# Weighted experts in 64x64 tiles: seven block products for both matrix products

## The chip, the cores and the metric

The kernel runs on one core of one Trainium2 chip. TensorE (PE) multiplies matrices into PSUM, VectorE (DVE) and ScalarE (ACT) work on PSUM and SBUF, GpSimd (POOL) on SBUF alone, and SyncE (SP) issues nearly all transfers (DMA). The metric is the time of one execution on the device in microseconds (us), the median of the runs.

## The reference

A linear attention feeds a mixture of eight experts whose weights come out of Sinkhorn iterations. N = 4352 tokens, D = 128, E = 8, F = 1024, all in float32.

```python
# attention: (4, 4, 1088, 32) inputs, features phi(x) = outer(S1 x, S2 x), 64 of them
num = q_p @ (k_p^T v);  den = q_p @ sum(k_p) + 1e-6
x = (num / den), heads side by side             # (4352, 128)
# experts
P = np.exp(x @ w_gate - max)
for _ in range(8):
    P /= P.sum(1, keepdims=True) + 1e-09
    P /= P.sum(0, keepdims=True) + 1e-09
    P *= N / E
for e in range(E):
    h = np.maximum(x @ w1[e], 0.0)              # (4352, 1024)
    out += P[:, e:e + 1] * (h @ w2[e])          # (4352, 128)
```

The weights P are positive, so `P * relu(x w1)` is the same as `relu((P x) w1)`.

## The kernel before

`xT` holds the attention's result with the 128 channels on the partitions and the tokens along the free dimension. The work of the experts is a list of `groups` (a stretch of tokens and a list of experts), and an item is one expert in one group. While the attention and the Sinkhorn iterations run on VectorE, TensorE is filled with plain items: experts 0 and 1 on tokens that need no weight yet; their sums are kept in `kept` and weighted later. The generator `steps()` yields after every step of expert work, and `fill(n)` runs some steps between two pieces of the other work.

The other items are weighted: `prepare_x` loads a row of P, broadcast to 128 partitions, and GpSimd multiplies the tokens by it (L682) ahead of the first product. Weighted groups of 768 tokens are three tiles of 256. `four` computes the first product directly (L918, ReLU on ScalarE, L922): four blocks of 128 hidden units by three tiles, each as two 128x64 matmuls on the two column halves of the array. `twenty` gives the second product (L1103) as 20 block products in place of 24, with sums of hidden blocks on VectorE (L982, L1002) and sums of weight blocks (`sums_of_four`, L246) that GpSimd computes once and SP stores and loads again (L234). The last group has two tiles of 256 and a scheme with seven products in place of eight (`two`, `seven`). The second products of a block are issued eight steps after its first products (`LAG`), between first products of later blocks, so that TensorE need not wait for ReLU and sums.

PSUM has eight banks: four rotate for first products (`aps`), four hold the sums of the second products (`mps`, tags s0 to s3). `load_w` brings an expert's w1 (L194) and w2 (L195, 512 KB each) through SP; the pool `wpool` has two buffers of each, so a load waits until the use before last of its buffer is over.

TensorE, VectorE and ScalarE run in the order in which the source issues (`manual_schedule(engines=...)`); SP and GpSimd are ordered by the scheduler, except where `keep_in_program_order` pins an instruction. Every engine carries out its instructions in its order; an instruction that waits holds up those behind it, and on SP these are transfers.

Of the kernel before, what the change touches and what calls it, by code (L numbers as in the profile page):

```python
# [50 lines left out]
def kernel(  # L51
# [33 lines left out]
    aps = ctx.enter_context(tc.tile_pool(name="aps", bufs=4, space=PSUM))  # L85
    mps = ctx.enter_context(tc.tile_pool(name="mps", bufs=1, space=PSUM))
    dram = ctx.enter_context(tc.tile_pool(name="dram", bufs=1, space=bass.MemoryType.DRAM))
# [103 lines left out]
    def load_w(e, sums=True, again=False):  # L191
        w1 = wpool.tile([P, F], F32, tag="w1", name="w1")
        w2 = wpool.tile([P, FO, DM], F32, tag="w2", name="w2")
        nc.sync.dma_start(out=w1, in_=moe_w1[e])  # L194
        nc.sync.dma_start(out=w2, in_=moe_w2[e].rearrange("(fo fi) d -> fi fo d", fi=P))  # L195
        return w1, w2, sums_of_two(e, w2, again) if sums else None

    def sums_of_two(e, w2, again=False):

        ws = wpool.tile([P, 4, FO // 2, H2], F32, tag="ws", name="ws")  # L200
        if e in stored:
            nc.sync.dma_start(out=ws, in_=stored[e])
            return ws
        a11, a21 = w2[:, 0::2, 0:H2], w2[:, 0::2, H2:DM]
        a12, a22 = w2[:, 1::2, 0:H2], w2[:, 1::2, H2:DM]
        keep_ = tc.keep_in_program_order if e < 2 else lambda x: x
        keep_(nc.gpsimd.tensor_tensor(ws[:, 0], a21, a22, op=Alu.add))
        keep_(nc.gpsimd.tensor_tensor(ws[:, 1], ws[:, 0], a11, op=Alu.subtract))
        keep_(nc.gpsimd.tensor_tensor(ws[:, 2], a11, a21, op=Alu.subtract))
        keep_(nc.gpsimd.tensor_tensor(ws[:, 3], a12, ws[:, 1], op=Alu.subtract))  # L210
        if again:
            stored[e] = dram.tile([P, 4, FO // 2, H2], F32, name=f"ws{e}")
            nc.sync.dma_start(out=stored[e], in_=ws)
        return ws

    stored, stored_four = {}, {}

    FOURS = (((5, 6), ((0, 0), (0, 2)), ((1, 0), (1, 2)), True),  # L220
# [7 lines left out]
    FORMS = [n for ns, *_ in FOURS for n in ns]  # L228

    def sums_of_four(e, w2):  # L230

        ws = pools[0].tile([P, len(FORMS), FO // 4, H2], F32, tag="ws4", name="ws4")
        if e in stored_four:
            nc.sync.dma_start(out=ws, in_=stored_four[e])  # L234
            return ws

        def blocks(bs):
            b = w2[:, bs[0][1]::4, H2 * bs[0][0]:H2 * (bs[0][0] + 1)].unsqueeze(1)
            if len(bs) == 1:
                return b  # L240
            step = (bs[1][1] - bs[0][1]) * DM + (bs[1][0] - bs[0][0]) * H2
            return AP(tensor=b.tensor, offset=b.offset, ap=[b.ap[0], [step, 2], *b.ap[2:]])

        c = 0
        for ns, x, y, off in FOURS:
            tc.keep_in_program_order(nc.gpsimd.tensor_tensor(ws[:, c:c + len(ns)], blocks(x), blocks(y),  # L246
                                                             op=Alu.subtract if off else Alu.add))
            c += len(ns)
        stored_four[e] = dram.tile([P, len(FORMS), FO // 4, H2], F32, name=f"ws4{e}")
        nc.sync.dma_start(out=stored_four[e], in_=ws)  # L250
        return ws


# [38 lines left out]
    first_w = load_w(0, False)  # L292
# [282 lines left out]
    def routing():  # L575
# [45 lines left out]
        for b in (1, 0, 2, 3):  # L621
# [10 lines left out]
    NT3 = 256  # L632

    groups = [(0, 256, 2, [0], False), (512, 288, 2, [0], False), (0, 256, 2, [1], False),
              *((1088 + 832 * i, 416, 2, [0], False) for i in range(3)), (3584, 384, 2, [0], False),
              (512, 384, 2, [1], False)]
    PLAIN = len(groups)


    DIRECT = (0,)
    for lo in (1280, 512, 2048, 2816, 3584):
        groups.append((lo, NT3, 3, list(range(2 if lo == 512 else 1, E)), True))
    groups.append((0, 256, 2, list(range(2, E)), True))
    assert sorted((lo, e) for lo, n, t, es, _ in groups for lo in range(lo, lo + n * t, 32) for e in es) == [
        (lo, e) for lo in range(0, N, 32) for e in range(E)]
    kept = [keep.tile([P, N], F32, name="kept0"), keep.tile([P, 1280], F32, name="kept1")]
    items = [(g, e) for g, group in enumerate(groups) for e in group[3]]
    loaded_w, sources, sums, parts, done = {}, {}, {}, {}, {}  # L650
# [5 lines left out]
    def tiles_of(j):  # L656
        return groups[items[j][0]][2]

    def prepare_w(j):
        g, e = items[j]  # L660
        three = groups[g][2] == 3
        if j == 0:
            loaded_w[j] = first_w
        elif items[j - 1][1] == e or not groups[g][4]:
            before = [i for i in range(j) if items[i][1] == e and i in loaded_w]
            loaded_w[j] = loaded_w[before[-1]] if before else load_w(e, False)
            if three and tiles_of(j - 1) == 2:
                loaded_w[j] = *loaded_w[j][0:2], sums_of_four(e, loaded_w[j][1])
        else:
            loaded_w[j] = load_w(e, not three, again=groups[g][4])  # L670
            if three:
                if g == len(groups) - 2 and e in groups[-1][3]:
                    sums_of_two(e, loaded_w[j][1], True)
                loaded_w[j] = *loaded_w[j][0:2], sums_of_four(e, loaded_w[j][1])

    def weights_of(e, lo, n, tag):
        pb = pools[0].tile([P, 3 * NT3], F32, tag=tag, name=tag)[:, 0:n]
        tc.keep_in_program_order(nc.sync.dma_start(out=pb, in_=pT[e:e + 1, lo:lo + n].to_broadcast([P, n])))
        return pb

    def weigh(out, x, pb):
        tc.keep_in_program_order(nc.gpsimd.tensor_tensor(out, x, pb, op=Alu.mult))  # L682

    def prepare_x(j):
        g, e = items[j]
        lo, n, t, es, weighted = groups[g]
        x = xT[:, lo:lo + t * n]
        if not weighted:
            sources[j] = x
            return  # L690
        xe = weights_of(e, lo, t * n, "xe")
        for sl in (slice(0, 512), slice(512, 768)) if j == first_weighted else (slice(0, t * n),):
            weigh(xe[:, sl], x[:, sl], xe[:, sl])
        sources[j] = xe

    first_weighted = next(j for j, (g, e) in enumerate(items) if g == PLAIN)

    def weigh_kept(g, i):

# [185 lines left out]
    LAG = 8  # L885
# [389 lines left out]
```

## Time and profile before

| | |
|---|---|
| runs | 920.46, 920.62 and 922.18 us; median 920.62 us |
| profiled execution | span 919.9 us, 19030 instructions |
| TensorE busy | 913.1 us, 99% |
| VectorE, ScalarE, GpSimd busy | 685.0 us (74%), 421.2 us (46%), 211.0 us (23%) |
| moved by DMA | 128.17 MB, 139 GB/s in the mean |

The profile is of one execution. Busy time is the time in which at least one instruction of an engine runs; the chain that ended last follows the end of the program back through what each instruction waited for. "PE" rows are matmuls, "PEld" rows weight loads. Line numbers are those of the kernel printed above.

### The profile page before, as it was taken

What the parts mean: (1) busy time and instruction counts of PE and PEld (TensorE: products, weight loads), DVE (VectorE), ACT (ScalarE), POOL (GpSimd) and SP (SyncE); (2) the same over time, 40 slices, a digit from 0 to 9 for tenths busy, and PEclk for the clock granted to TensorE, in tenths of its full rate; (3) what the DMA queues carried; (4) which work ended last, traced back from release to release, by engine and by line L of the source; (5) the groups of instructions that cost most, each with busy time, mean ns of one, the idle gap of its engine ahead of it and who ended that gap; (6) DMA issues with size and microseconds to landing.
All of it is one profiled execution on the core that took longest, in us unless ns stands there. A gap on an engine that the chain in (4) does not pass through costs nothing.

```text
span 919.9 us, 19030 instructions
## 1 busy us (share of the span) xinstructions
PE 913.1 (99%) x7510; PEld 596.8 (65%) x7510; DVE 685.0 (74%) x1173; ACT 421.2 (46%) x915; POOL 211.0 (23%) x212
## 2 busy tenths in 40 slices
PE   9999999999999999999999999999999999999997
PEld 5777544466666666666666666666666666668665
DVE  7678699888776798756985666967667986668665
ACT  2455465554444454444544444544445444446443
POOL 3121100076545412200210011110100352221220
PEclk9999999999999999999999999999999999999999
DMA  8995100213554535534364343464435556453650
GB/s 233 309 276 178 53 1 1 70 64 116 157 142 147 169 136 152 187 109 139 121 173 148 110 149 110 125 196 120 139 114 169 155 149 195 157 170 92 176 152 13
DMA packets 91306, 128.17 MB, mean 139 GB/s; under 512 B 25392, under 2 KB 69504, under 8 KB 86480
## 3 DMA queue, kind: packets, MB, share of 16 engines
q1 hardware_dynamic: 88384, 121.42, 42.7%
q0 software_dynamic: 1600, 5.36, 1.9%
q8 instruction: 59, 0.97, 0.4%
q10 hardware_dynamic: 1232, 0.16, 0.1%
q14 instruction: 31, 0.25, 0.1%
HBM read 107.88 MB, written 19.05 MB: 138 GB/s over the span
## 4 chain that ended last, share of the span: by engine, by line
PE 98%; DVE 1%; issue 0%; ACT 0%; POOL 0%; DVEq 0%; POOLq 0%
PE a L918 56%; PE s L1103 37%; PE a L351 1%; PE a L117 1%; PE a L466 1%; PE a L318 0%; PE s L380 0%; DVE hb L935 0%; PE a L430 0%; PE s L396 0%; PE a L500 0%; PE a L396 0%; DVE cs L606 0%; DVE rs L600 0%; DVE y L794 0%
## 5 line engine op out<-in xcount | busy, mean ns | idle before, releaser
L918 PE MATMUL a<-xe,w 128*64 128x256 f32 (+1 forms) x2560 | 692.1, 470 | 0.0
L918 PEld LDWEIGHTS a<-xe,w 128*64 128x64 f32 x2560 | 320.4, 137 | 112.8 <-issue 1.6
L1103 PE MATMUL s<-hb,ws 128*64 128x256 f32 (+3 forms) x1312 | 331.6, 395 | 0.2 <-DVE hb L935 0.2
L1103 PE MATMUL s<-hx,ws 128*64 128x256 f32 x1280 | 306.3, 379 | 0.0
L922 ACT ACTIVATE hb<-a 128x256 f32<-128x256 f32 (+4 forms) x408 | 195.0, 480 | 241.9 <-PE a L918 208.9
L922 ACT ACTIVATE hx<-a 128x256 f32<-128x256 f32 (+1 forms) x360 | 167.0, 464 | 213.6 <-PE a L918 191.3
L982 DVE TENSOR_TENSOR hb<-hb 128x512 f32<-128x512 f32 (+1 forms) x204 | 134.9, 671 | 100.9 <-ACT hb L922 97.0
L1103 PEld LDWEIGHTS s<-hb,ws 128*64 128x64 f32 x1312 | 158.4, 137 | 70.2 <-issue 14.2
L982 DVE TENSOR_TENSOR hx<-hx 128x512 f32<-128x512 f32 (+1 forms) x204 | 152.7, 759 | 59.8 <-ACT hx L922 54.7
L682 POOL TENSOR_TENSOR xe<-xT,xe 128x768 f32<-128x768 f32 (+2 forms) x41 | 85.0, 2074 | 481.6 <-DMA xe<-pT 371.3
L1103 PEld LDWEIGHTS s<-hx,ws 128*64 128x64 f32 x1280 | 154.5, 137 | 57.3
L1103 PE MATMUL s<-hb,w 128*64 128x256 f32 (+3 forms) x536 | 134.4, 408 | 0.0
L918 PE MATMUL a<-xT,w 128*64 128x416 f32 (+3 forms) x512 | 119.9, 463 | 0.0
L1103 PE MATMUL s<-hx,w 128*64 128x256 f32 x384 | 95.7, 380 | 0.0
L1103 PEld LDWEIGHTS s<-hb,w 128*64 128x64 f32 x536 | 60.5, 137 | 23.4 <-issue 6.5
L935 DVE TENSOR_TENSOR hb<-hb 128x416 f32<-128x416 f32 (+7 forms) x84 | 60.7, 723 | 18.7 <-ACT hb L922 14.8
L918 PEld LDWEIGHTS a<-xT,w 128*64 128x64 f32 x512 | 49.5, 137 | 25.1 <-issue 15.5
L246 POOL TENSOR_TENSOR ws<-w 128x256 f32<-128x256 f32 (+1 forms) x70 | 62.1, 920 | 5.4 <-DMA w<-in_moe_w_dram 4.0
L935 DVE TENSOR_TENSOR hx<-hx 128x256 f32<-128x256 f32 (+1 forms) x65 | 38.6, 598 | 24.7 <-ACT hx L922 23.6
L1103 PEld LDWEIGHTS s<-hx,w 128*64 128x64 f32 x384 | 46.1, 137 | 11.8 <-DVE hx L935 0.7
L982 DVE TENSOR_TENSOR pqg<-hb 128x512 f32<-128x512 f32 x68 | 46.5, 723 | 0.0
L982 DVE TENSOR_TENSOR pqg<-hx 128x512 f32<-128x512 f32 x68 | 36.4, 574 | 0.0
(181 smaller groups left out, 483.0 us busy)
## 6 DMA issues: line engine op xcount, KB each, us to landing
w<-in_moe_w_dram SPq DMA_DIRECT2D x82, 512.0 KB, 5.6
ws<-ws SPq DMA_DIRECT2D x34, 1024.0 KB, 5.0
xe<-pT SPq DMA_DIRECT2D x34, 384.0 KB, 4.0
ws<-ws SPq DMA_DIRECT2D x12, 512.0 KB, 4.3
ph<-qa SPq DMA_DIRECT2D x12, 288.0 KB, 5.0
rb<-qb SPq DMA_DIRECT2D x3, 1152.0 KB, 7.8
pb<-pT SPq DMA_DIRECT2D x6, 384.0 KB, 7.2
kx<-in_k_dram SPq DMA_DIRECT2D x4, 544.0 KB, 5.2
```

The costliest lines, as they stand in the source:

```text
L117: nc.tensor.matmul(warm[r][cols, 0:256], ones[rows, cols], ones[rows, 0:1].to_broadcast([64, 256]), start=True, stop=True, tile_position=( ...
L246: tc.keep_in_program_order(nc.gpsimd.tensor_tensor(ws[:, c:c + len(ns)], blocks(x), blocks(y), op=Alu.subtract if off else Alu.add))
L351: nc.tensor.matmul(pv[64 * s:64 * (s + 1), i], kp[0:n, H * t + h].rearrange("p i j -> p (i j)"), vx[0:n, slots[h], t, :], start=(t == 0 an ...
L466: nc.tensor.matmul(pn[64 * s:64 * (s + 1), t, 2 * i:2 * i + 2].rearrange("p h d -> p (h d)"), ph[:, i, s, 64 * t:64 * (t + 1)], kvs[b % 2] ...
L682: tc.keep_in_program_order(nc.gpsimd.tensor_tensor(out, x, pb, op=Alu.mult))
L918: nc.tensor.matmul(ph[sl], loaded_w[j][0][:, P * f + H2 * s:P * f + H2 * (s + 1)], sources[j][:, lo:hi], start=True, stop=True, tile_posit ...
L922: nc.scalar.activation(out=out, in_=ph, func=Act.Relu)
L935: nc.vector.tensor_tensor(out, a, b, op=Alu.subtract)
L982: nc.vector.tensor_tensor(out if not isinstance(out, tuple) else places(*out), places(*a), places(*b) if isinstance(b, tuple) else b, op=A ...
L1103: nc.tensor.matmul(sums[g][i][H2 * s:H2 * (s + 1), n * place:n * (place + 1)], w, x, start=c == 1, stop=c == per, tile_position=(0, H2 * s))
```

## The change

The plain items stay. `twenty`, `four` and the last group's scheme go, and after the plain items a new phase runs, `weighted()`, with all engines in the order of the source. Its items are nine groups `wgroups`, each of two tiles of n tokens (six of n = 256, two of 224, one of 192) with six or seven experts; every second group takes its experts in reverse order, so that the expert at a border stays. All matmuls are 64x64 with four positions in the array. An item is done in two halves s.

- First product: channels, hidden units and tokens are each cut in two, and seven products of blocks replace eight. `w1x` holds 4 raw blocks of w1 and 4 sums (`sum_forms`, GpSimd, at an expert's first use; then `store_forms` stores them, and `stored_forms` loads 1 MB of them and 512 KB of `ws`). `xf` holds the weighted tokens (`weigh`, GpSimd), a copy with the partition halves exchanged (two DMAs from SBUF to SBUF), and four sums (`sum_x`, VectorE). The products accumulate in two pairs of PSUM banks; the state in between is copied out or added (`firsts`).
- Second product: seven products again, with sums `ts` of hidden blocks (`seconds`), summed over an item's rounds and a group's experts in the four banks of `mps`. In the first weighted group the second product is plain, eight products.
- One round of `firsts` of half t and one of `seconds` of half t - 1 alternate on TensorE.
- A group's end: copies out of PSUM, a sum, an exchange of partition halves by DMA, nine small adds, the kept sums, transposes, stores; the VectorE part runs in pairs at `spare()`.

```diff
+    wgroups = [*((1280 + 512 * i, 256, list(range(1, E))) for i in range(6)),
+               (0, 224, list(range(2, E))), (448, 224, list(range(2, E))), (896, 192, list(range(2, E)))]
...
+    def stored_forms(e):
+        w1 = late[0].tile([P, 8, FORM], F32, tag="w1x", name="w1x")
+        w2 = wpool.tile([P, FO, DM], F32, tag="w2", name="w2")
+        ws = wpool.tile([P, 4, FO // 2, H2], F32, tag="ws", name="ws")
+        nc.sync.dma_start(out=w1, in_=form_stores[e][0])
+        nc.sync.dma_start(out=w2, in_=moe_w2[e].rearrange("(fo fi) d -> fi fo d", fi=P))
+        nc.sync.dma_start(out=ws, in_=form_stores[e][1])
+        return w1, w2, ws
...
+    def load_weights(i):
+        g, e = witems[i]
+        lo, n, _ = wgroups[g]
+        weights[i] = late[0].tile([P, 2 * NW], F32, tag="pb", name="pb")[:, 0:2 * n]
+        nc.sync.dma_start(out=weights[i], in_=pT[e:e + 1, lo:lo + 2 * n].to_broadcast([P, 2 * n]))
+
+    def weigh(i):
+
+        lo, n, _ = wgroups[witems[i][0]]
+        xf = sources[i] = late[0].tile([P, 8 * NW], F32, tag="xf", name="xf")[:, 0:8 * n].rearrange(
+            "p (b n) -> p b n", b=8)
+        nc.gpsimd.tensor_tensor(xf[:, 0:2].rearrange("p b n -> p (b n)"), xT[:, lo:lo + 2 * n], weights.pop(i),
+                                op=Alu.mult)
+        for s in range(2):
+            nc.sync.dma_start(out=xf[H2 * (1 - s):H2 * (2 - s), 2:4], in_=xf[H2 * s:H2 * (s + 1), 0:2])
+
+    def sum_x(i, part_):
+        xf = sources[i]
+        if part_ == 0:
+            nc.vector.tensor_tensor(xf[:, 4:6], xf[:, 1:4:2], xf[:, 0:2], op=Alu.subtract)
+        else:
+            nc.vector.tensor_tensor(xf[:, 6], xf[:, 3], xf[:, 4], op=Alu.subtract)
+            nc.vector.tensor_tensor(xf[:, 7], xf[:, 2], xf[:, 6], op=Alu.subtract)
+
+    def prepare(i):
+
+        if i < len(witems):
+            e = witems[i][1]
+            if i and witems[i - 1][1] == e:
+                forms[i] = forms[i - 1]
+            else:
+                forms[i] = stored_forms(e) if e in form_stores else raw_forms(e)
+
+    def begin(i):
+        if i >= 0:
+            store_forms(i)
+        else:
+            load_weights(0)
+        prepare(i + 1)
+        if i + 2 < len(witems):
+            load_weights(i + 2)
+        if i + 1 < len(witems):
+            weigh(i + 1)
+            if witems[i + 1][1] not in form_stores:
+                sum_forms(forms[i + 1])
+        if i >= 0:
+            weigh_kept(i)
...
+        def firsts(t):
...
+            def product(out, form, x, start, stop):
+                for r in range(2):
+                    rows = slice(H2 * r, H2 * (r + 1))
+                    for col in range(2):
+                        o = P * s + H2 * col
+                        nc.tensor.matmul(out[H2 * col:H2 * (col + 1), r], w1[rows, form, o:o + H2], xf[rows, x],
+                                         start=start, stop=stop, tile_position=(H2 * r, H2 * col), skip_group_check=True)
...
+            product(pa, 0, 0, True, True)
+            nc.scalar.copy(flat(p1, n), pa)
+            yield
+            product(pc, 4, 4, True, True)
+            nc.scalar.copy(flat(p5, n), pc)
+            yield
+            product(pa, 5, 6, False, True)
+            nc.scalar.copy(flat(u2, n), pa)
+            yield
+            product(pc, 7, 3, False, True)
+            add(h[:, 0], pc, u2)
+            relu(h[:, 0], h[:, 0])
+            yield
+            product(pa, 6, 5, False, True)
+            add(h[:, 2], pa, p5)
+            relu(h[:, 2], h[:, 2])
+            yield
+            product(pc, 2, 2, True, True)
+            add(h[:, 3], pc, p1)
+            if i + 1 < len(witems):
+                sum_x(i + 1, s)
+            spare()
+            if g == 0:
+                relu(h[:, 3], h[:, 3])
+            yield
+            product(pa, 3, 7, False, True)
+            relu(flat(h[:, 1], n), pa)
+            if g:
+                nc.vector.scalar_tensor_tensor(ts[:, 0:2], h[:, 3:4].to_broadcast([P, 2, 2 * n]), 0.0, h[:, 0:2],
+                                               op0=Alu.max, op1=Alu.subtract)
+                nc.vector.tensor_tensor(ts[:, 2], h[:, 1], ts[:, 0], op=Alu.subtract)
+                nc.vector.tensor_tensor(ts[:, 3], h[:, 2], ts[:, 2], op=Alu.subtract)
+            yield
...
+            for m, (x, y) in enumerate((((raw, (0, 0), h[:, 0], 0, 0), (raw, (0, 1), h[:, 2], 0, 0)),
+                                        ((form, (3,), h[:, 1], 0, 1), (form, (0,), ts[:, 0], 0, 1)),
+                                        ((form, (2,), ts[:, 1], 1, 0), (form, (1,), ts[:, 2], 1, 0)))):
+                for r in range(2):
+                    both(into(0, x[0](*x[1], r), x[2], r, *x[3:]), into(1, y[0](*y[1], r), y[2], r, *y[3:]))
+                    if last and m == 1 and r == 1:
+                        ended(g, 0)
+                    yield
+            both(into(0, raw(1, 1, 0), ts[:, 3], 0, 1, 1), into(1, raw(1, 1, 1), ts[:, 3], 1, 1, 1))
...
+        for t in range(len(todo) + 1):
+            if t < len(todo) and todo[t][1] == 0:
+                begin(todo[t][0])
+            f = firsts(t) if t < len(todo) else iter(())
+            s = seconds(t - 1) if t else iter(())
+            nothing_, open_ = object(), 2
+            while open_:
+                open_ = sum(next(x, nothing_) is not nothing_ for x in (f, s))
+        while leisure:
+            leisure.pop(0)()
...
-        pools.append(ctx.enter_context(tc.tile_pool(name="late", bufs=2)))
-        prepare_x(PLAIN)
-        fill(8)
-    for _ in work:
-        pass
+        late.append(ctx.enter_context(tc.tile_pool(name="late", bufs=2)))
+        begin(-1)
+        fill(7.5)
+        for _ in work:
+            pass
+        sum_x(0, 0)
+        sum_x(0, 1)
+    turning.close()
+    fps = ctx.enter_context(tc.tile_pool(name="fps", bufs=1, space=PSUM))
+    with tc.manual_schedule():
+        weighted()
```

More of the change, by code (lines that the diff above doesn't have):

```diff
@@ L676, in weights_of @@
[L676 to L694, printed above, removed]
@@ L1105, in into @@
+        nc.tensor.matmul(sums[g][i][H2 * s:H2 * (s + 1)], w, x, start=c == 1, stop=c == per,
+                         tile_position=(0, H2 * s))
         if c == per:
@@ L1108, in into @@
                 part(g, i)
-    def second(k, p):
-        into(items[blocks[k][0]][0], *p)
     def steps():
@@ L1137, in steps @@
                     loaded_w.update({i: w for i in loaded_w if items[i][1] == items[j + 1][1]})
[L1138 to L1145 removed]
+                step, sums_ = two(k)
+                products = eight if g in DIRECT else seven
+            for c in range(4):
                 if k < len(blocks):
@@ L1152, in steps @@
                 for b, p in todo.pop(t, ()):
-                    second(b, p)
+                    into(items[blocks[b][0]][0], *p)
                 if k < len(blocks) and c == 0:
@@ L1163, in steps @@
                         later.pop(0)()
-                elif later and (tiles == 3 or c % 2 or share > 0.9):
+                elif later and (c % 2 or share > 0.9):
                     later.pop(0)()
```

549 lines of the change are left out of this document (222 added, 327 removed), and 7 rows, old and new, of the table FOURS.

## The prediction, made before the changed kernel ran

> **What bounds the kernel now.** I read the page first: the busy times, then the chain that ended last, then the costliest groups.
>
> ```profile
> PE 913.1 (99%) x7510; PEld 596.8 (65%) x7510; DVE 685.0 (74%) x1173; ACT 421.2 (46%) x915; POOL 211.0 (23%) x212
> ...
> PE 98%; DVE 1%; issue 0%; ACT 0%; POOL 0%; DVEq 0%; POOLq 0%
> ...
> L918 PE MATMUL a<-xe,w 128*64 128x256 f32 (+1 forms) x2560 | 692.1, 470 | 0.0
> ```
>
> TensorE is busy for 913.1 us, the chain runs through it for 98%, and its main group never waited. So two things move the end: TensorE work taken away, and any wait put in front of TensorE. The mean of 470 ns is no price, since matmuls overlap; the price is the distance between starts, in TensorE's timeline near the end:
>
> ```profile
> 908.96 1.03 PE L1103 MATMUL s<-hx,ws 128*64 128x256 f32 x8
> 909.82 1.03 PE L1103 MATMUL s<-hb,w 128*64 128x256 f32 x8
> 910.68 0.38 PE L1103 MATMUL s<-hx,ws 128*64 128x256 f32 x1
> ```
>
> Eight instructions take 0.86 us. One matmul of the source is two instructions (the x2560 are 1280 calls), and two column halves run side by side, so a pair of 128x64 matmuls over 256 columns costs 0.43 us. I call that a round.
>
> **TensorE's work.** The weighted phase before has 34 items of 768 tokens, each of two blocks with 12 rounds of first and 10 of second products; 6 items of 512 tokens, four blocks of 4 + 3.5 rounds; and 2.5 rounds more that go into the last sums: 1496 + 180 + 2.5 = 1678.5 rounds, 721.8 us.
>
> Afterwards a round is four 64x64 matmuls. That four run at once only the warm-up shows, in the timeline of the start:
>
> ```profile
> 1.00 8.17 PE L117 MATMUL a<-ones 64*64 64x256 f32 x96 [1.00 <-POOL own L120]
> ...
> 5.75 0.25 PEld L117 LDWEIGHTS a<-ones 64*64 64x64 f32 x4 [0.18 <-issue]
> ...
> 6.17 0.25 PEld L117 LDWEIGHTS a<-ones 64*64 64x64 f32 x4 [0.18 <-issue]
> ...
> 6.60 2.11 PEld L117 LDWEIGHTS a<-ones 64*64 64x64 f32 x40 [0.18 <-issue]
> ```
>
> From 6.60 on, 40 loads take 2.11 us, 0.42 us for the eight instructions of four matmuls. I keep 0.43. A half item costs 7 rounds of first and 7 of second products (8 in the first group, whose second products are plain): 14 x 15 + 35 x 28 = 1190 rounds of 256 columns, 336 of 224 and 168 of 192, worth 1610 rounds, 692.3 us. TensorE's work falls by **29.5 us**, if nothing new waits.
>
> **The wait that the change adds.** Take item i with its halves A and B. At the start of A, `begin(i)` puts on SP's queue, in this order (the new region keeps every engine in the order written, SP and POOL too): w1's forms for item i+1, w2, the sums `ws`, the weights `pb` of item i+2, and only then the two transfers that swap the halves of `xf` for item i+1. w2 has two buffers. The one that item i+1 gets was item i-1's, and the second products of i-1's last half run between the first products of this very half A, down to A's last round. SP does wait for such releases; its own waits:
>
> ```profile
> SPq L234 <- PE s L1103: 153.4, 23, 7.7
> ...
> SPq L195 <- PE s L1103: 49.8, 30, 7.3
> ```
>
> L195 loads w2; it was held 30 times until second products let a buffer go. So SP will stand at w2 until the end of A (call it moment 0), and behind it stand `ws`, `pb` and the swaps. VectorE's program, which is in order, has `sum_x(i+1, 0)` after A's sixth round of first products, and that reads the swapped half. So VectorE stands from before moment 0 until the swap lands, and behind it stand the four sums `ts` of half A. TensorE does five rounds of half B (2.15 us) and then, in its third round of second products, needs the first of these sums.
>
> When does the swap land? SP's spacing and a burst with a like number of bytes are in SP's timeline, the windows beside it and the DMA issues:
>
> ```profile
> 490.09 0.32 SPq L678 DMA_DIRECT2D xe<-pT  x1
> 490.46 0.42 SPq L194 DMA_DIRECT2D w<-in_moe_w_dram  x1
> 498.67 0.32 SPq L234 DMA_DIRECT2D ws<-ws  x1
> 499.96 0.38 SPq L195 DMA_DIRECT2D w<-in_moe_w_dram  x1
> ```
> ```profile
> 499.50:500.00 0.50, 0.50 (x6) 0.29 (x4) 0.50 (x2) 0.38 (x1) 0.00 (x0) 1.00 0.55 66
> ...
> 505.00:505.50 0.50, 0.50 (x6) 0.35 (x4) 0.18 (x1) 0.00 (x0) 0.00 (x0) 1.00 0.11 33
> 505.50:506.00 0.50, 0.50 (x6) 0.28 (x4) 0.00 (x0) 0.39 (x1) 0.00 (x0) 1.00 0.00 0
> ```
> ```profile
> w<-in_moe_w_dram SPq DMA_DIRECT2D x82, 512.0 KB, 5.6
> ws<-ws SPq DMA_DIRECT2D x34, 1024.0 KB, 5.0
> ```
>
> The last columns of a window are the granted clock, the DMA share and GB/s. 1024 KB of sums and 512 KB of w2 kept the DMA engines busy until about 505.4, 6.7 us after the first issue. Afterwards the burst is w2 512, `ws` 512, `pb` 256 and the swaps 256 KB, the same total, with the swaps at its end. With 0.1 us for SP to wake, the landing is at 6.8 us. Bounds come from the tile `xd`, the transfer out of SBUF that this trace has, below with the rows of the engines' steps:
>
> ```profile
> DMA to landing us min/median/max: 2.4/3.3/7.9
> ```
> ```profile
> L982 DVE TENSOR_TENSOR hx<-hx 128x512 f32<-128x512 f32 x136 | 98.6, 725 | 47.4 <-ACT hx L922 44.2
> L335 DVE TENSOR_TENSOR kp<-ab 128x1024 f32<-128x1024 f32 x8 | 9.6, 1216 | 2.0 <-ACT ab L321 2.0
> L935 DVE TENSOR_TENSOR hx<-hx 128x256 f32<-128x256 f32 x42 | 20.9, 500 | 1.8 <-ACT hx L922 0.7
> ```
> ```profile
> L922 ACT ACTIVATE hx<-a 128x512 f32<-128x512 f32 x136 | 81.2, 597 | 103.4 <-PE a L918 85.4 <-DVE hb L982 13.7 <-DVE hx L982 3.3
> ```
> ```profile
> L682 POOL TENSOR_TENSOR xe<-xT,xe 128x512 f32<-128x512 f32 x7 | 10.2, 1451 | 124.9 <-PE s L1103 79.8 <-DMA xe<-pT 30.9 <-PE a L918 14.2
> ```
>
> Early end: the fifth issue, 0.1 + 4 x 0.37 = 1.6 us, and 2.4 us, so 4.0; late end: 7.9. I take 6.8, the precedent of the same size. Then VectorE does `sum_x` (512 wide, 0.73 us) and the first pair of `ts` (1024 wide, 1.22 us); with 0.2 us of handing over TensorE goes on at 8.95. It stopped at 2.15, so **6.8 us of idle TensorE in one item**; 4.0 by the early end, 7.9 by the late one.
>
> How many items? Of 59 preparations, 7 keep the expert across a border of groups, the 7 after them find the buffer free earlier, and so does the first. That leaves 44: 5 in the first group, 26 in the next five, 13 in the last three, where smaller tiles give about 6.6. In the first group no `ws` is loaded and no `ts` exists: the late step is the add of half B's first sum, needed after ten rounds (4.3 us) and ready at about 6.7; 3 us with the stores of the new forms in the same queue. Together 26 x 6.8 + 13 x 6.6 + 5 x 3 = **278 us**. Between `sum_x` and `ts` stand also up to two adds of a finished group, 0.4 to 0.5 us each, in about three stalled items after each of six borders: 18 x 0.85 = **15 us**.
>
> The rest hides: POOL's product ahead of the swap (1.45 us) is done while SP stands, and after the stop 23 rounds lie before the next moment 0, in which VectorE catches up. With that cover gone POOL's product would add its 1.45 us per item.
>
> **The clock.** An idle TensorE is clocked down, as the windows at the end show:
>
> ```profile
> 914.00:915.00 1.00, 0.93 (x9) 0.35 (x5) 0.93 (x4) 0.00 (x0) 0.00 (x0) 1.00 0.00 0
> 917.00:918.00 1.00, 0.00 (x0) 0.00 (x0) 0.00 (x0) 0.00 (x0) 0.00 (x0) 0.98 0.90 130
> 918.00:919.00 1.00, 0.00 (x0) 0.00 (x0) 0.00 (x0) 0.00 (x0) 0.00 (x0) 0.50 0.32 45
> ```
>
> The last matmul ends at 914.9 and the clock is halved at 918.0, 3 us later. The start shows the way back: groups of four came every 0.42 us (5.75, 6.17), and every 0.21 us only from 6.60 on, 5.6 us after the first matmul. A stop of 6.8 us is therefore followed by some 5.6 us at half speed, which loses 2.8 us: 39 x 2.8 = **109 us** (none for the first group's 3 us). Bounds: 0, if the clock should hold, and 39 x 3.4 if the way back took as long as the stop.
> The Trainium skill (TensorE: Matmul & The Clock Gate, Part 1) says that a free-running window of about 3.4 us decides: halved after one idle window, restored after one busy one. By that rule the slow stretch is 3.4 to 6.8 us, 5.1 in the mean, and the term 39 x 2.55 = 99 us in place of 109; this trace's 3 and 5.6 us agree with it.
>
> **The edges.** The phases no longer overlap. VectorE must do the last plain adds (about four) and `sum_x` before the second round, some 4.6 us for TensorE; the first half has no second products between its rounds and the last no first ones: 2.6 us. At the end, this is what now lies behind the last matmul:
>
> ```profile
> 913.69 1.24 PE L1103 MATMUL s<-hb,w 128*64 128x256 f32 x9
> ...
> 915.92 0.45 DVE L718 STREAM_TRANSPOSE yt<-y 128x256 f32<-128x256 f32 x1
> ```
>
> Before: 5.0 us from 914.93 to the span's end, 3.6 of them the stores. Afterwards: copies 1.0, a sum 0.5, a swap 3, nine adds 3.5, two adds and two transposes 1.4, stores 3.6: 13, so 8 us more. Edges: **15 us**.
>
> **The sum**, on the profiled execution of 919.9 us: 919.9 - 29.5 + 278 + 15 + 109 + 15 = 1307.4; the median of the runs is 0.7 us above that span, so **1308 us**.
>
> **Rivals.**
> - The swap is not late: were the slot of w2 free, or the swap issued ahead of it, so that it lands by moment 0, nothing stops. For it: POOL is 77% idle and SP's work per item is short. Against it: the 30 waits of L195. VectorE would then have 3 x 0.73 + 0.73 + 1.22 + 2 x 0.73 = 5.6 us in a half of 6.02, so TensorE stays the bound: 919.9 - 29.5 + 15 + 0.7 = 906 us, faster. It decides if the sums are ready at 2.15, that is, if the swap lands by 0.1 us after moment 0. Chance 0.05.
> - The stop is there, but the clock holds: 1199 us. For it: only one drop and one rise are in the trace, and 3 us is half the stop. Chance 0.15.
> - The swap doesn't queue behind the burst and lands at 4.0: a stop of 4.0 us, 39 x 2.8 = 109 us less, and a clock that drops in some stops only: 1090 to 1199, say 1150. For it: sixteen DMA engines take several transfers at once. Against: a total of 1.5 MB shares them. Chance 0.13.
> - Four tiles with four different inputs don't run at once (the warm-up streams a single repeated column): rounds of 0.86 us, 692 us more work and, as the sums are then needed at 4.3 us, stops of 4.7 us: about 1900 us. Chance 0.03.
>
> **How the numbers follow.** The forecast has 0.62 and spans 1210 to 1380: the late end gives 39 x 1.1 = 43 us more, slower VectorE steps some 20. The remaining 0.02 is for what I don't see. The range 1110 to 1380 holds the forecast, the held clock and most of the third rival. A measurement of this kernel can tell about 0.2% from no change. Faster by more: the first rival, 0.05. Within: 0.01. Slower: 0.94.
>
> **What would show it.** In the changed profile: SP's waits should list w2 behind TensorE's second products some 40 times at about 6 us; VectorE's longest waits should be for the DMA into `xf`, 44 times; TensorE's busy share should fall to about 60 to 70%, with stops once in every item of 20 to 22 us, at the third round of second products; granted clocks of 0.7 to 0.9 in the slices; rounds of 0.43 us between stops. Wrong would be: no such waits on `xf` (then 906), full clock in every slice (1199), rounds well over 0.43 at full clock.

## The result and the profile after

The changed kernel takes **1445.04 us** (median of 4 runs, 1438.3 to 1450.18); the kernel before took 920.58 us. The ratio is 1.568, 95% interval 1.564 to 1.573. The forecast was 1308 us: the direction was right, but the time lies 137 us above the forecast and 65 us above the top of the range.

The page of the changed kernel, where before TensorE stood at 99% and the chain ran through it for 98%:

```profile
span 1436.4 us, 35651 instructions
...
PE 1025.1 (71%) x15436; PEld 751.4 (52%) x15436; DVE 845.5 (59%) x1264; ACT 536.5 (37%) x993; POOL 163.6 (11%) x197
...
PEclk9999998998878897888889887978787879789777
...
PE 49%; DVE 21%; DMA 18%; SPq 6%; issue 4%; ACT 2%; POOL 0%; DVEq 0%; ACTq 0%; POOLq 0%
```

No engine is busy throughout, the clock dips in nearly every slice of the second phase, and VectorE and a transfer have joined the chain. The waits name them (engine and line, what was waited for; us in total, times, longest), first the engines, then SP:

```profile
DVE xf L905 <- DMA xf<-xf: 384.3, 44, 10.3
PE s L1051 <- DVE hb L1023: 361.6, 69, 10.7
```
```profile
SPq L855 <- PE s L1051: 125.8, 22, 7.7
SPq L855 <- PE pair L981: 111.5, 24, 7.1
```

L905 is `sum_x(i+1, 0)`: it waited for the swap 44 times, the number that the prediction counted. L855 loads w2: SP was held there 46 times. One item in the timeline (start, duration; in brackets the idle time before and what ended it):

```profile
704.45 0.40 SPq L855 DMA_DIRECT2D w<-in_moe_w_dram  x1
...
706.05 1.25 SPq L900 DMA_DIRECT2D xf<-xf  x2
...
706.28 0.59 PE L1051 MATMUL s<-hb,ws 64*64 64x256 f32 x2
713.38 0.69 DVE L905 TENSOR_TENSOR xf<-xf 128x512 f32<-128x512 f32 x1 [9.53 <-DMA xf<-xf]
...
714.35 1.18 DVE L1023 SCALAR_TENSOR_TENSOR hb<-hb 128x1024 f32<-128x1024 f32 x1
...
715.59 0.69 PE L1051 MATMUL s<-hb,ws 64*64 64x256 f32 x3 [8.72 <-DVE hb L1023]
```

SP wakes at w2, issues `ws`, `pb` and then the two swaps; VectorE goes on 8.93 us after w2's issue; TensorE stood 8.72 us. Such an idle time of TensorE is a stop below. The windows of the same item (length, then busy PE, PEld, DVE, ACT, POOL, granted clock, DMA share, GB/s) show the clock:

```profile
706.00:707.00 1.00, 0.87 (x14) 0.33 (x5) 0.00 (x0) 0.92 (x2) 0.00 (x0) 1.00 0.70 196
707.00:711.50 4.50, 0.00 (x0) 0.00 (x0) 0.00 (x0) 0.25 (x1) 0.00 (x0) 1.00 0.92 294
711.50:712.00 0.50, 0.00 (x0) 0.00 (x0) 0.00 (x0) 0.00 (x0) 0.00 (x0) 0.79 0.07 29
712.00:716.00 4.00, 0.41 (x4) 0.31 (x8) 2.59 (x4) 0.00 (x0) 0.00 (x0) 0.50 0.11 19
716.00:718.50 2.50, 2.50 (x28) 1.45 (x24) 1.64 (x3) 0.09 (x1) 0.00 (x0) 0.50 0.20 30
719.00:720.00 1.00, 1.00 (x27) 0.72 (x19) 0.75 (x2) 0.19 (x2) 0.00 (x0) 1.00 0.00 0
```

It fell at 711.8, when TensorE had stood for 4.9 us, and came back at about 718.6. The mechanism of the forecast is there, place by place; its sizes are not.

### The profile page after: what moved, and what is told of

Same layout as the page of the kernel before. It is cut to its first block, busy times and chain, and to the rows that moved or that the text cites. A ratio compares the mean times of both kernels' runs of the same rounds, so it can differ in the third digit from the quotient of the medians.

```text
span 1436.4 us, 35651 instructions
## 1 busy us (share of the span) xinstructions
PE 1025.1 (71%) x15436; PEld 751.4 (52%) x15436; DVE 845.5 (59%) x1264; ACT 536.5 (37%) x993; POOL 163.6 (11%) x197
## 4 chain that ended last, share of the span: by engine, by line
PE 49%; DVE 21%; DMA 18%; SPq 6%; issue 4%; ACT 2%; POOL 0%; DVEq 0%; ACTq 0%; POOLq 0%
PE s L1051 20%; DMA xf<-xf 18%; PE pair L981 18%; DVE hb L1023 7%; PE a L705 4%; PE s L766 4%; DVE xf L908 4%; DVE hb L985 3%; DVE y L1094 2%; DVE z L1094 2%; SPq L856 2%; SPq L890 2%; SPq L900 2%; DVE xf L907 1%; DVE hb L720 1%
## 5 line engine op out<-in xcount | busy, mean ns | idle before, releaser
L981 PE MATMUL pair<-xf,w1x 64*64 64x256 f32 (+2 forms) x6720 | 706.6, 399 | 28.6 <-DVE hb L985 20.1
L1051 PE MATMUL s<-hb,ws 64*64 64x256 f32 (+2 forms) x3392 | 441.5, 428 | 362.9 <-DVE hb L1023 361.6
L1051 PEld LDWEIGHTS s<-hb,ws 64*64 64x64 f32 x3392 | 246.6, 157 | 445.7 <-DVE hb L1023 401.9
L981 PEld LDWEIGHTS pair<-xf,w1x 64*64 64x64 f32 x6720 | 387.3, 146 | 108.0 <-issue 27.4
L988 ACT ACTIVATE hb<-hb 128x512 f32<-128x512 f32 (+2 forms) x254 | 155.0, 610 | 633.2 <-DVE hb L985 627.5
L985 DVE TENSOR_TENSOR hb<-pair,copies 128x512 f32<-128x512 f32 (+2 forms) x360 | 238.0, 663 | 137.4 <-PE pair L981 132.2
L1051 PE MATMUL s<-hb,w 64*64 64x256 f32 (+2 forms) x3440 | 300.3, 373 | 0.2 <-ACT z L1091 0.2
L905 DVE TENSOR_TENSOR xf<-xf 128x512 f32<-128x512 f32 (+2 forms) x60 | 40.8, 680 | 384.3 <-DMA xf<-xf 384.3
L1051 PEld LDWEIGHTS s<-hb,w 64*64 64x64 f32 x3440 | 175.4, 136 | 35.7 <-issue 4.5
L999 ACT COPY copies<-pair 128x512 f32<-128x512 f32 (+2 forms) x120 | 68.1, 568 | 36.1 <-PE pair L981 36.1
L1002 ACT COPY copies<-pair 128x512 f32<-128x512 f32 (+2 forms) x120 | 67.7, 564 | 31.6 <-PE pair L981 31.6
L996 ACT COPY copies<-pair 128x512 f32<-128x512 f32 (+2 forms) x120 | 68.0, 567 | 30.7 <-PE pair L981 29.1
L1025 DVE TENSOR_TENSOR hb<-hb 128x512 f32<-128x512 f32 (+2 forms) x106 | 71.1, 671 | 3.7
L1026 DVE TENSOR_TENSOR hb<-hb 128x512 f32<-128x512 f32 (+2 forms) x106 | 70.2, 662 | 3.6
```

The costliest lines, as they stand in the source:

```text
L981: nc.tensor.matmul(out[H2 * col:H2 * (col + 1), r], w1[rows, form, o:o + H2], xf[rows, x], start=start, stop=stop, tile_position=(H2 * r, ...
L985: nc.vector.tensor_tensor(flat(out, n), x, flat(y, n), op=Alu.add)
L988: nc.scalar.activation(out=x, in_=y, func=Act.Relu)
L1025: nc.vector.tensor_tensor(ts[:, 2], h[:, 1], ts[:, 0], op=Alu.subtract)
L1026: nc.vector.tensor_tensor(ts[:, 3], h[:, 2], ts[:, 2], op=Alu.subtract)
L1051: yield lambda rho=rho, rows=rows, c=c: nc.tensor.matmul(acc[g][rho][q][H2 * half:H2 * (half + 1), n * place:n * (place + 1)], w[rows], fl ...
```

## The experiments

The question in three parts. Theory: SP is held at w2's buffer, and the swaps stand behind the hold and behind the bytes issued ahead of them. Rivals: the traffic alone, whatever its order; or VectorE at its limit. Then: what the clock costs, and what is left once the long stops are gone. Runs e5 to e8 are from another chip than the rest; the kernel before took 921.6 us there and 921.4 and 921.9 beside the others.

**1. The order, the buffers and the bytes.** Swaps first:

```diff
+        if i + 1 < len(witems):
+            weigh(i + 1)
         prepare(i + 1)
...
-            weigh(i + 1)
```

> In begin(i) the product and the two swaps of xf for item i+1 are put on SP's queue ahead of the loads of item i+1. Theory (SP is held at w2's buffer, and the swaps stand behind it): the 44 long stops (367 us) and the clock lost with them (93 us) go; 1436 - 460 = 976 us, and VectorE's waits on xf in the waits view fall from 384 us to under 40. What stays are the short stops of 0.3 to 1.2 us (some 35 us). Rival 1 (traffic: the swaps share the DMA engines with the 1024 KB of w1's forms that are issued just behind them, whatever the order): landing 6 us or more after the item's start, stops of 2 to 3 us in most items and a clock that drops in some, 1080 us or more. Rival 2 (VectorE cannot keep up: 11 us of work per item of 12 us, held by GpSimd): TensorE stops 2 us or more per item for ts, not for xf, 1050 us or more.

1030.86 us (1026.44 to 1032.7), ratio 1.118 [1.115, 1.121]. Its waits on the swap:

```profile
DVE xf L905 <- DMA xf<-xf: 68.1, 38, 4.9
```

414 us and nearly all long stops are gone: five over 2 us are left after the first group, 17 us together. So the order in SP's queue makes the stops; neither rival holds as it was put, although w1's megabyte is issued right behind the swaps. But 1031 is not 976: some 60 shorter stops, 47 us, are left, and VectorE still waits 68 us for the swap, where under 40 were expected. The third part follows that up.

Three buffers of w2 and `ws`, the order as it was:

```diff
+        loads[0] += 1
+        pool, more = (late[0], dict(bufs=1)) if loads[0] % 3 == 0 else (wpool, {})
+        w2 = pool.tile([P, FO, DM], F32, tag="w2", name="w2", **more)
+        ws = pool.tile([P, 4, FO // 2, H2], F32, tag="ws", name="ws", **more)
...
-        w2 = wpool.tile([P, FO, DM], F32, tag="w2", name="w2")
-        ws = wpool.tile([P, 4, FO // 2, H2], F32, tag="ws", name="ws")
+        w2, ws = w2_and_ws()
```

> w2 and ws of the weighted phase get three buffers in turn in place of two; the order in SP's queue is as it was. If the hold at w2's buffer alone makes the stops, they go: about 976 us, as with the swaps first. My theory has two parts, the hold and the bytes ahead: with three buffers SP's waits on second products go (237 us in the waits view to under 20), but w1's forms, w2, ws and pb (2.25 MB) are then issued together at the item's start, when the last first product lets w1's buffer go, and the swaps land some 10 us after that; ts is needed 8.2 us after the item's start, so stops of about 4.5 us are left in 44 items: 1436 - 367 - 93 + 198 + some 90 for the clock = 1265 us.

1294.16 us (1293.12 to 1295.82). SP no longer waits for second products at w2, but 38 stops of 5.8 us in the mean are left, where 4.5 were expected. What SP still stands at is w1's buffer, as in the changed kernel (287 us there):

```profile
SPq L861 <- PE pair L988: 316.8, 27, 17.4
```

When that comes free, at the start of an item, w1's forms, w2, `ws`, `pb` and the swaps go out together. Taking the hold at w2 away without the order gains 151 us of the 414: now the bytes are ahead.

`ws` and `pb` behind the swaps, the hold kept:

```diff
-        nc.sync.dma_start(out=ws, in_=form_stores[e][1])
+        ws_loads.append(lambda: nc.sync.dma_start(out=ws, in_=form_stores[e][1]))
...
         prepare(i + 1)
+        if i + 1 < len(witems):
+            weigh(i + 1)
+        while ws_loads:
+            ws_loads.pop(0)()
```

> SP's order is w1's forms, w2, swaps, ws, pb: the hold at w2 stays, 768 KB (ws, pb) go behind the swaps. By the bytes ahead of them the swaps land some 4.9 us after the hold ends in place of 8.4 us, stops of 5.3 us in place of 8.7 to 9.2 in the 39 items after the first group, the clock still drops in each: 1436 - 39 x 3.5 = 1300 us. Rival (all bytes under way share the DMA engines alike, whatever their order): landing as before, 1420 to 1440 us. Rival (the hold counts, bytes hardly): also about 1420 to 1440 us; the two are told apart by the three buffers.

1365.91 us (1362.55 to 1371.98), 79 us less where 145 were expected. The 39 stops are 6.8 us long in the mean, not 5.3; what is still ahead is w2:

```profile
644.40 0.38 SPq L856 DMA_DIRECT2D w<-in_moe_w_dram  x1
...
644.88 1.18 SPq L901 DMA_DIRECT2D xf<-xf  x2
...
650.42 0.69 DVE L906 TENSOR_TENSOR xf<-xf 128x512 f32<-128x512 f32 x1 [6.61 <-DMA xf<-xf]
```

The hold with only an eighth of w2 ahead; the rest of w2, `ws` and `pb` follow the swaps:

```diff
+        nc.sync.dma_start(out=w2[:, 0], in_=rows[:, 0])
+        rest.append(lambda: nc.sync.dma_start(out=w2[:, 1:FO], in_=rows[:, 1:FO]))
...
+        rest.append(lambda: nc.sync.dma_start(out=ws, in_=form_stores[e][1]))
...
         prepare(i + 1)
+        if i + 1 < len(witems):
+            weigh(i + 1)
+        while rest:
+            rest.pop(0)()
```

> The hold stays, nearly all bytes behind it go: of w2 only one eighth (64 KB) is loaded ahead of the swaps, and the other seven eighths, ws and pb come behind them. The swaps then land as soon after the hold as they do with nothing ahead, about 3.0 us for the pair, and sum_x starts 3.5 us after SP wakes in place of 8.4 (6.9 with all of w2 ahead): stops of about 4 us in the 39 items, 1436 - 39 x 4.8 = 1250 us, and 10 to 40 us less where the clock's drops get shorter: 1210 to 1250 us. If the bytes matter whatever their order: 1350 us or more. If the hold is not what counts but only the bytes: 1000 us or less.

1244.32 us (1240.66 to 1253.23), as expected; 38 stops of 4.2 us in the mean. In its timeline:

```profile
711.42 0.33 SPq L839 DMA_DIRECT2D w<-in_moe_w_dram  x1
...
711.85 1.11 SPq L906 DMA_DIRECT2D xf<-xf  x2
...
714.85 0.69 DVE L911 TENSOR_TENSOR xf<-xf 128x512 f32<-128x512 f32 x1 [4.03 <-DMA xf<-xf]
```

Set side by side, from the first issue after the hold to `sum_x`: 3.43 us with the hold alone, 6.02 with all of w2 ahead, 8.93 with `ws` and `pb` too. These are the three items shown; the means over the 38 or 39 items after the first group are 4.2, 6.8 and 8.3 us. So of the 414 us that the order costs, with the bytes taken away first, the bytes make 201 (1445 against 1244; w2 has 122 of them, `ws` with `pb` 79) and the hold 213 (1244 against 1031). The shares depend on that sequence: with the hold at w2 taken away first, it gives 151.

The swaps on GpSimd's own queue:

```diff
-            nc.sync.dma_start(out=xf[H2 * (1 - s):H2 * (2 - s), 2:4], in_=xf[H2 * s:H2 * (s + 1), 0:2])
+            nc.gpsimd.dma_start(out=xf[H2 * (1 - s):H2 * (2 - s), 2:4], in_=xf[H2 * s:H2 * (s + 1), 0:2])
```

> The two swaps of xf are issued on GpSimd's own DMA queue behind its product; SP's queue is otherwise as it was, w2 is still held there. Theory (queue order): the swaps are issued 1.3 us after the item's start and share the DMA engines with w1's forms; they land 4 to 6 us after the start, in time or nearly: 960 to 1020 us. Rival (the transfer itself is slow among the other traffic): stops of 3 us or more remain, 1150 us or more.

1072.5 us (1064.89 to 1078.94): SP is held at w2 as before, 46 times, and the long stops go all the same. That confirms the theory, but the time is 50 us above the expected range: 13 stops over 2 us stayed after the first group, 55 us. Ahead of ten of them GpSimd had stood 11 to 14 us for a row of P (`pb` or `pk`), which still comes through SP's queue, so that its product and the swaps were late.

**2. The clock.** 16 rounds of matmuls that no later step reads stand where TensorE would be idle. They start new accumulations in the pairs' banks, so this kernel's hidden sums are not the reference's; only its times are read.

```diff
+                for _ in range(16):
+                    for r in range(2):
+                        for col in range(2):
+                            rows = slice(H2 * r, H2 * (r + 1))
+                            nc.tensor.matmul(pairs[0][H2 * col:H2 * (col + 1), r, 256:256 + n],
+                                             w1[rows, 0, H2 * col:H2 * (col + 1)], xf[rows, 0], start=True, stop=True,
+                                             tile_position=(H2 * r, H2 * col), skip_group_check=True)
```

> The changed kernel with 64 more matmuls (16 rounds, 6.9 us, into columns of the pairs that nobody reads) in each item that stops, just ahead of the third second products of half B, where TensorE would stand idle for 7.3 to 12 us. The sums arrive no earlier or later. If the clock is lowered because TensorE is idle, the idle rest of 1 to 4 us is too short for most drops: of the 93 us that the clock cost, some 75 to 85 come back, 1350 to 1365 us, mean granted clock above 0.95. Rival (the clock follows something else than idle time): 1436 us or more and a clock of 0.86.

1404.79 us (1400.96 to 1408.44), mean clock 0.956 against 0.861. TensorE's waits for `ts` fall by 246 us, about what was put in; VectorE's stay:

```profile
DVE xf L905 <- DMA xf<-xf: 387.8, 43, 10.7
...
PE s L1051 <- DVE hb L1023: 115.3, 67, 8.3
```

So idle time lowers the clock, and the rival falls. But 40 us came back, not 75 to 85. The loss is half of TensorE's busy time in the stretches at half clock: 93 us before and 47 with the filling. 24 of 44 such stretches stayed: stops of 2.1 us and more that were left over still dropped the clock, and those of the first group were not filled. I had taken 3 us as safe.

**3. What is left without the long stops.** First one suspect in the changed kernel itself: GpSimd's product, held back to the third first product of half A by a tiny addition (the gate) that reads its copy.

```diff
+    def middle(i, u2):
         if i + 1 < len(witems):
+            gate = late[0].tile([P, 8], F32, tag="gate", name="gate", bufs=1)
+            nc.gpsimd.tensor_tensor(gate, u2[:, 0:8], u2[:, 0:8], op=Alu.add)
             weigh(i + 1)
...
+            if s == 0:
+                middle(i, u2)
```

The sums of the forms and the weighing of the kept output, which follow the product, move with it.

> The changed kernel with one thing more: GpSimd's product for item i+1 waits (by a tiny addition that reads it) for the copy of half A's third first product. It is still done before SP's hold ends, so the long stops stay as they are. If the short second stop of each item comes from VectorE's 128x256 difference that is held beside GpSimd's product (1.46 in place of 0.42 us), these stops go: 30 to 40 us less, 1395 to 1410 us. Rival (VectorE is late because it has to catch up after the long stop): no change, 1430 to 1445 us.

1433.17 us (1429.75 to 1442.58): 12 us less, with ranges that overlap, not 30 to 40; the time alone lies in the rival's range. What the theory says of VectorE is nevertheless plain in the groups by form (times, busy us, mean ns; idle before), the changed kernel first, then the gated one:

```profile
L985 DVE TENSOR_TENSOR hb<-pair,copies 128x512 f32<-128x512 f32 x252 | 173.3, 690 | 107.0 <-PE pair L981 104.8
...
L908 DVE TENSOR_TENSOR xf<-xf 128x256 f32<-128x256 f32 x42 | 51.3, 1221 | 1.4
```
```profile
L991 DVE TENSOR_TENSOR hb<-pair,copies 128x512 f32<-128x512 f32 x252 | 172.9, 690 | 109.1 <-PE pair L987 106.2
...
L908 DVE TENSOR_TENSOR xf<-xf 128x256 f32<-128x256 f32 x42 | 17.9, 425 | 1.4
```

The difference of 128x256, beside GpSimd's product, took 1221 ns in the mean and takes 425 without it; the adds out of PSUM take 690 ns in both, though GpSimd now works beside them. But VectorE's gain reached TensorE only in part: stops of 0.3 to 2.2 us fell from 29 to 21 us, and the loss by the clock grew from 93 to 100 us. The 29 us were of another kind: 26.5 of them came behind that difference and leftover adds together. Of the 21 us, 8 come behind leftover adds, and 12 are new. Where SP isn't held, the product that is held back makes the swap itself late, as the number of waits shows (44 in the changed kernel):

```profile
DVE xf L905 <- DMA xf<-xf: 400.3, 57, 10.6
```

So the second stop of the changed kernel did come from the difference, and the gate paid for its removal with new waits.

Then, from the swaps first, everything an item ahead: three `xf` buffers, GpSimd weighs item i+2, its swaps stand between w1's forms and w2, `sum_x` in two halves of two items.

```diff
-                sum_x(i + 1, s)
+            if s == 0 and i + 1 < len(witems):
+                if i == 0:
+                    sum_x(1, 0)
+                sum_x(i + 1, 1)
+            if s == 1 and i + 2 < len(witems):
+                sum_x(i + 2, 0)
```

> Product, swaps and sums of x run a whole item ahead: three xf buffers; in item i GpSimd weighs item i+2, its swaps stand on SP's queue between w1's forms and w2 of item i+1, and sum_x(i+2) is half in B of item i, half in A of item i+1. No wait on a transfer into xf should be left (68 us with the swaps first), nor the 4 us stops where GpSimd stood at the kept weights: about 30 to 40 us less than with the swaps first, 990 to 1000 us. GpSimd's product still starts when the last first product of half B lets an xf buffer go, beside VectorE's 256-wide difference and the first sums ts, so the short stops stay (rival: if these came from the late swaps after all, they go here and the time is 930 us or less).

981.71 us (980.49 to 984.01), ratio 1.066 [1.064, 1.067]; the waits on the swap fall to 2 us. With the gate on top:

```diff
         if i + 2 < len(witems):
+            gate = late[0].tile([P, 8], F32, tag="gate", name="gate", bufs=1)
+            nc.gpsimd.tensor_tensor(gate, u2[:, 0:8], u2[:, 0:8], op=Alu.add)
             weigh(i + 2)
```

> As with everything an item ahead, and GpSimd first does a tiny addition that reads the copy of the third first product of half A, so that its product runs beside VectorE's three adds out of PSUM and not beside operations that read only SBUF. If VectorE's operations on SBUF are held while GpSimd works, the 128x256 difference falls from about 1.4 us back to 0.42 us, the first sums are in time and most short stops go: 30 to 45 us less than ungated, 945 to 965 us. Rival (VectorE is simply at its limit, 10.9 us of 12.0 per item and more in the narrow groups): within 10 us of the ungated kernel.

962.38 us (959.44 to 966.04), 19 us less; the rival allowed 10, the theory wanted 30. So the product's place has a share; whether VectorE's limit makes up the rest is not shown. The leftover adds behind `ts`, and one in a half in place of two:

```diff
-                for _ in range(2):
+                for _ in range(2 if g == 0 or len(leisure) > 14 else 1):
...
-            spare()
...
                 nc.vector.tensor_tensor(ts[:, 3], h[:, 2], ts[:, 2], op=Alu.subtract)
+                spare()
```

> As the gated one, and the leftover adds of an ended group go behind the sums ts, one in a half in place of two ahead of ts. Two adds of 0.42 us ahead of ts are what makes ts late in half B after a border: 15 to 25 us less than the gated one, 925 to 945 us. Rival: the adds then delay the next half's adds out of PSUM by as much, no gain.

983.99 us (983.79 to 988.72), 22 us more. TensorE's waits, gated and then with the adds later:

```profile
PE s L1063 <- DVE hb L1035: 9.7, 10, 2.6
PE pair L987 <- DVE hb L991: 8.1, 11, 1.7
```
```profile
PE pair L987 <- DVE hb L991: 20.7, 24, 5.0
...
PE s L1064 <- DVE hb L1035: 4.6, 8, 1.3
```

The waits for `ts` halve, those for the next half's adds out of PSUM more than double: the rival was right. It does not cover all of the 22 us: VectorE's waits on the swap also grow, from 5.1 to 22.4 us, and TensorE's on w1's forms from 1.3 to 7.0. The first item's sums ahead of the first phase's last adds, on top of that:

```diff
-        fill(7.5)
+        fill(6.0)
+        sum_x(0, 0)
+        sum_x(0, 1)
         for _ in work:
             pass
-        sum_x(0, 0)
-        sum_x(0, 1)
```

> As the one before, and the first item's sum_x stands ahead of the first phase's last adds: of the stop at the transition (5 to 6 us) some 4 to 5 us go, 920 to 940 us. The floor by work is 193 + 692 + 15 + 6 = 906 us; the kernel before is at 921 us. Rival: the swap of the first item is not there by then, VectorE stands and the first phase's products wait: no gain or up to 5 us more.

984.26 us (980.76 to 985.39): no gain, as its rival had it. The stop of 4.9 us at the transition gives way to others of 1.6 to 1.8 us. Last, on the gated kernel with everything an item ahead, one leftover add in a half (two while more than 14 are left) and the kept output's weighing right behind the gated product:

```diff
-                for _ in range(2):
+                for _ in range(2 if len(leisure) > 14 else 1):
...
             weigh(i + 2)
+        weigh_kept(i - 1)
```

> As the gated kernel with everything an item ahead, with one leftover add in a half in place of two (still ahead of ts), and the kept output's weighing an item later, right behind GpSimd's gated product, so that it meets fewer of VectorE's operations on SBUF. The pairs of adds make ts or the next adds late at the borders, and the weighing held VectorE there: 10 to 20 us less, 940 to 952 us. Rival: VectorE, at some 10.9 of 12.0 us per item, cannot make up for one add in every half either, so many small stops in place of few larger ones: 958 to 966 us.

954.92 us (952.42 to 955.54), ratio 1.035 [1.034, 1.037], 3 us above the expected range and the best version. Its largest stop, 7.9 us, waits for the exchange of a group's end, which again stands late in SP's queue. None beats the kernel before: the floor by work is 906 us, and a share of 1.6% is all that the fewer rounds could bring.

## Why the prediction was wrong

The terms beside what the profiled execution shows (stops: TensorE idle, from the trace):

| term | forecast, us | measured, us |
|---|---|---|
| TensorE's rounds | -29.5 | -26 (at the medians, 0.432, 0.379 and 0.325 us at 256, 224 and 192 columns) |
| 39 stops after the first group, leftover adds in them | 278 | 334 (39 x 8.57) |
| 5 stops in the first group | 15 | 19.5 (3.3 to 4.7) |
| second, short stops | 0 | 29 (36 of 0.3 to 1.2) |
| clock | 109 | 93 |
| edges | 15 | 16 (transition 6.2; end 15.2 in place of 5.0) |
| not named | 0 | 51 |

With 919.9 this is 1307.4 on the left and 1436.4 on the right. From start to start, the trace names most of the 51 us: 26 are the 0.3 us that each of 84 stops, long and short, costs beyond its idle time, and 21 are rounds at full clock, which took 0.446 us in the mean at 256 columns, not the median of 0.432. What lengthens these rounds stays open.

- **Mechanism: right**, as the waits (44, 46), the place (third round of second products in half B) and the swaps put first show. Rounds of 0.43 us, full clock between, settle the rival of four tiles that don't run at once. The clock did not hold.
- **The step that failed is the landing**, the largest term that was mis-sized; the next is "the rest hides", below. "I take 6.8, the precedent of the same size": the stops were 8.57 us long in place of 6.8, which is 56 of the 129 us that the sum was short. `sum_x` started 8.3 us after w2's issue in the mean of the 39 items (6.9 to 9.7). The trace divides this time. The burst was through but for a tail (DMA share under 0.2) 7.2 us after w2's issue in the mean, not far from the precedent's 6.7. The tail took some 0.5 us more; in the item shown the share from 711.5 on is 0.07, about one engine of sixteen. And VectorE starts about 0.6 us after the last packet, whose end I had taken as the landing. In 15 of the 39 items, moreover, 170 KB or more of w1's forms, which I had left out of the burst, were still moving: 8.7 us there, 8.0 in the others. The second swap was issued 2.3 us after w2 in the mean, where I had 1.5.
- Bytes alone do not price such a wait: by the means of experiment 1 the 512 KB of w2 ahead cost 2.6 us (6.8 against 4.2), the 768 KB of `ws` and `pb` 1.5 us (8.3 against 6.8). I added up bytes and did not ask which transfer they belong to; why w2's cost more is not tested.
- The early bound, 4.0, was the right price of another case: with the hold alone the stop is 4.2 us. "The swap doesn't queue behind the burst" had the stop right for that case, but its time is 1244 and not 1150: the clock drops there in almost every stop too and loses 82 us, and short stops, which that rival left out as well, take 35.
- **"The rest hides" failed.** POOL's product was costed by its own length and SP's wait. Beside it VectorE's difference took 1.46 us in place of 0.42, the sums of half B came late, and together with the leftover adds that gave most items a second stop. It is also part of why the rival of a swap in time was priced too low: 906 us counts VectorE's steps at their undisturbed lengths, 5.6 of 6.02 us; the chip needed 1031 with the swaps first and 955 after four more repairs.
- **The clock** came out near its term for partly wrong reasons: the first group's stops, costed at nothing, dropped it in four of five cases, and of 389 us at half clock only 186 fell on busy time, since the slow stretch begins inside the stop; I had 39 x 5.6 = 218.
- **The range** took the late bound of the landing as its edge and gave the short stops nothing. Without the 29 us of second stops and the 51 us of the last row the time would lie inside it, at some 1365 us, even with stops of 8.57 us.

## What to carry to other kernels

Put transfers that an in-order engine waits for ahead of loads whose buffer is not free, and price a landing by what stands before it in the queue, transfer by transfer, not by the sum of bytes. Another buffer helps only in part where the bytes then move ahead of the small transfer: 151 us of 414 here. Where VectorE fills nine tenths of TensorE's time, cost each of its operations beside GpSimd before calling anything hidden, and test a saving of 1.6% against one late wait per item.

## What the runs showed of the hardware

- An operation of VectorE with both inputs in SBUF that starts while GpSimd's product runs stands until the product ends: 425 ns alone, some 1460 beside it for 128x256. One with an input in PSUM does not, 690 ns either way. It depends on who is first: with everything an item ahead, VectorE's difference of 128x512 was under way already in nine items when the product began. It kept its 680 ns, and the product took up to 1467 ns, where 1280 is usual. The Trainium skill (SBUF — State Buffer, Who interferes with whom) says that a VectorE instruction with two SBUF inputs contends with a GpSimd instruction that reads SBUF, and that the ports they share are an exclusive lock; the rows above agree.
- The clock is halved for multiples of 3.41 us: in the changed kernel 28 stretches of 10.2, 14 of 6.8 and 2 of 3.4 us, beginning 2.0 to 5.1 us after a stop does. All stops of 3.29 us and more were followed by one, and one of 3.27 us was not; in the filled kernel some of 2.1 us were, and one of 2.9 was not. The Trainium skill (TensorE: Matmul & The Clock Gate, Part 1) gives a free-running window of 3.4 us and one idle window as the condition; the lengths agree, but a stop of 2.1 us cannot hold a whole idle window, nor can the 3.0 us after which the clock fell at the end of the kernel before, which the prediction took as agreement. A window that is idle for the larger part was enough: on the grid of 3.41 us on which the clock's changes lie, TensorE was idle for 56% or more of the window ahead of each drop in these two kernels, and for 59% at most in a window of the second phase without one.
